# A Fourier mixing layer and a low-rank mixer in one kernel: batch 0's transposed operand by TensorE, batch 1's transform two slots on and interleaved, later steps moved

## The chip, the cores and the metric

The kernel runs on one core of one Trainium2 chip. The metric is the device time of one execution in microseconds (us), as the median of several runs. The core has five engines with a program each: TensorE (PE, with its weight loads as PEld), VectorE (DVE), ScalarE (ACT), GpSimd (POOL) and SyncE (SP), which issues most DMAs. They wait for each other by semaphores. An instruction that waits holds everything behind it on its engine.

## The reference

Batch 8, sequence 3136, width 256, all float32. `x` is Fourier-transformed along both axes and the real part kept; then a mixer follows that has a low-rank product along the sequence (rank 32) and two channel products (256 to 1024 to 256) with a relu between.

```python
X = np.fft.fft(x, axis=1)
X = np.fft.fft(X, axis=2)
x = X.real                                   # (8, 3136, 256)
xt = x.transpose(0, 2, 1)
h = xt @ U @ V                               # U: 3136 x 32, V: 32 x 3136
u = x + h.transpose(0, 2, 1)
ch = np.maximum(u @ w_ch1, 0.0) @ w_ch2
return u + ch
```

## The kernel before

**The transform of a batch.** The 3136 rows are folded on DVE with their mirror rows (`fold`: `alone`, `along_d`, `mirror`, `half`, `fourth`; tiles xf and xr hold the rows forward and reversed, eof, eor, eos, ge, gc and go the folded ones). The folded rows are multiplied on PE with tables of sines and cosines that the kernel makes itself. There are four such products per batch, each in two halves (`pn` 0 and 1): even cosine rows (`a` in `transform`), odd cosine rows (`c`), even sine rows (`s`) and odd sine rows (`d`). They collect in PSUM tiles `pt`; half 0 is copied out by ACT to a tile `ev`, and sums and differences of the two halves (`mirrored`, `apart`, `join`) go to the tiles A (cosine) and B (sine). From A and B, `chan(b, ch, h)` makes the transform along the width: a PSUM tile `pst`, copied to S (`h` 0) or T (`h` 1). Four pairs (`ch` 0 to 3) fill a batch's 1568 + 1 rows; the other half of the rows follows from them by symmetry.

**The low-rank part.** The products also yield the transform of U's columns, in the tile `tab`. `lowrank(b)` multiplies it with the width's table (`MDT`: MSN and MC) to `ptt`, 128 x 256. ACT copies that to TA (with two columns repaired) and a second time, as it is, to TX, and a transposing DMA on SP brings TX to TD. `hidden(b, hh)` multiplies TD with W1 to `pq`, copied to QF.

**The chunks.** The 8 x 1568 rows are worked in 25 chunks of 512. `front(c, hf)` makes a chunk's u for the rows (`hf` 0) and the mirrored rows (`hf` 1): two PSUM tiles `ph` from TA and V, added on DVE to S and T; a transposing DMA brings u to ut. `direct(c, q)` multiplies u with W1 into four PSUM tiles `p1`; ACT applies the relu (L722). `mirrors(c, q)` adds WD and DV products with QF to the same tiles for the mirrored rows, and ACT applies the relu again (L738). `second_product` multiplies with W2; DVE adds ut and writes `o` (L781, L782), POOL repairs two columns, and `store` sends it out. `odd_part` makes uo = S - T on DVE.

**PSUM.** Tag dft has two buffers, taken in turn by `pt` (of `even_rows` and `seq`), `ptt`, `pst`, `pq` and `ph`; p1 has four, p2 two.

**The order.** Up to `order.close()` the order is as written. After it, the order on PE and that of the folds on DVE is as written (`keep_in_program_order`), and a scheduler places the rest, ACT's and DVE's evictions, POOL's and SP's instructions, around them. Each chunk has six slots: `turn(c, 0)` to `turn(c, 5)`, so slot n is `turn(n // 6, n % 6)`. A table `due` says which steps of later batches' transforms stand in which slot. `transform(b)` gives a first slot and a list of steps per slot; the fold steps of batch b are spread over the slots from `last` on up to it; `chan` 2 and 3 stand in four slots from 6 * (b * 1568 // 512) on. The folds of batch b also issue the loads of batch b + 1 (`load_part`). `front(c + 1, 0)` stands between slots 4 and 5 of chunk c, `front(c, 1)` between slots 1 and 2; batch 1 is first needed by `front(3, 0)`, behind slot 16.

Every PE instruction of this part comes through the helper `mm` (L427), every fold through `fold_tt` (L422).

Of the kernel before, what the change touches and what calls it, by code (L numbers as in the profile page):

```python
# [11 lines left out]
FP32 = mybir.dt.float32  # L12
# [4 lines left out]
P = 128  # L17
# [9 lines left out]
QW = TE + NE  # L27
# [4 lines left out]
def kernel(  # L32
# [9 lines left out]
    nc = tc.nc  # L42
# [4 lines left out]
    HALF = S // 2  # L47
    CH = 512
# [4 lines left out]
    psum = ctx.enter_context(tc.tile_pool(name="psum", bufs=1, space=bass.MemoryType.PSUM))  # L53
# [58 lines left out]
    EB = 4  # L112
    BUFS = {"dft": 2, "p1": 4, "p2": 2}
# [5 lines left out]
    wp = ctx.enter_context(tc.tile_pool(name="wp", bufs=2))  # L119
# [74 lines left out]
    TD = [cpool.tile([P, 2, P], BF16, name=f"td{s}", tag=f"td{s}") for s in range(2)]  # L194
# [194 lines left out]
    def along_d(qs, src, dst, part):  # L389
        lo, hi = src[:, qs, :, 1:128], src[:, qs, :, 255:128:-1]  # L390
        if part == 0:
            fold_tt(dst[:, qs, :, 1:128], lo, hi, op=AL.subtract)
        else:
            fold_tt(dst[:, qs, :, 129:256], lo, hi, op=AL.add)

    def alone(qs, src, dst, eng=None):

        (eng or nc.gpsimd.tensor_copy)(dst[:, qs, :, 128:257:128], src[:, qs, :, 0:129:128])

    def mirror(nm, cols, op):  # L400
        if nm == 0:
            fold_tt(EOS[:, 0, :, :, cols], EOF_[:, 0:4:2, :, cols],
                                    EOR_[:, 3::-2, ::-1][:, :, :, cols], op=op)
        else:
            fold_tt(EOS[:, 1, :, :, cols], EOR_[:, 0:4:2, ::-1][:, :, :, cols],
                                    EOF_[:, 3::-2, :, cols], op=op)

    def half(b, par, cols):
        dst = GE if par == 0 else GO[b % 2]
        fold_tt(dst[:, :, :, cols], EOS[:, :, 0, :, cols], EOS[:, :, 1, :, cols],  # L410
                                op=AL.add if par == 0 else AL.subtract)

    def fourth(b, c, cols):
        fold_tt(GC[b % 2][c][:, :, cols], GE[:, 0, :, cols], GE[:, 1, :, cols],
                                op=AL.add if c == 0 else AL.subtract)
# [10 lines left out]
    def mm(*a, **k):  # L426
        ins = nc.tensor.matmul(*a, **k)  # L427
        if len(pinned) > 1:
            tc.keep_in_program_order(ins)
        if pinned:  # L430
            pinned.append(ins)
# [3 lines left out]
    def fold(b):  # L435

        for nm, (qf, qr) in enumerate(((EV, OD), (OD, EV))):
            yield lambda qf=qf: (alone(qf, xf, EOF_), along_d(qf, xf, EOF_, 0))
            yield lambda qf=qf: along_d(qf, xf, EOF_, 1)
            if b > 1:  # L440
                yield lambda qr=qr: (alone(qr, xr, EOR_), along_d(qr, xr, EOR_, 0))
                yield lambda qr=qr: along_d(qr, xr, EOR_, 1)
            if b + 1 < B:
                yield lambda qf=qf, qr=qr, nm=nm: load_part(b + 1, nm)
            yield lambda nm=nm: mirror(nm, slice(0, 128), AL.subtract)
            yield lambda nm=nm: mirror(nm, slice(128, 258), AL.add)
        yield lambda: half(b, 0, slice(0, 258))
        yield lambda: (fourth(b, 0, slice(0, 258)), fourth(b, 1, slice(0, 258)))
        yield lambda: half(b, 1, slice(0, 258))

    def load_part(b, nm):

        for q in (0, 2) if nm == 0 else (1, 3):
            load_f(x, xf, b, q, D)
        load_r(x, xr, b, 1 - nm, 2, D)
        if nm == 1:
            load_0(x, xf, xr, b, D)

    def state(b):

        if b not in ST:
            d = ST[b] = {}
            d["A"] = wp.tile([P, HALF + 1], BF16, tag="A", name="A", bufs=1)
            d["B"] = wp.tile([P, HALF + 1], BF16, tag="B", name="B", bufs=1)
            d["tab"] = wp.tile([P, 2, 2, P], BF16, tag="tab", name="tab", bufs=1)
            d["S"] = wp.tile([P, HALF + 1], BF16, tag="S", name="S", bufs=2)
            d["T"] = wp.tile([P, HALF + 1], BF16, tag="T", name="T", bufs=2)
        return ST[b]
# [79 lines left out]
    def even_rows(b, typ, pn, tag="dft"):  # L548

        d = state(b)  # L550
        ne = NE if b else 0
        if pn == 0:
            d["pt"] = psum.tile([P, QW], FP32, tag=tag, name="pt", bufs=BUFS[tag])
        pt = d["pt"]
        todo = products(b, 0, typ, P * typ, pn == 1, ne)
        if typ == 0:
            todo = todo + products(b, 0, 1, 256, pn == 0, ne)
        for n, (at, w, rhs) in enumerate(todo):
            mm(pt[:, at:at + rhs.shape[-1]], w, rhs, start=(pn == 0 and n == 0),
               stop=(n == len(todo) - 1), skip_group_check=True)  # L560
        if pn == 0:
            ev = d["ev"] = wp.tile([P, QW], FP32, tag="ev", name="ev", bufs=EB)
            nc.scalar.copy(ev[:, :TE + ne], pt[:, :TE + ne])
            return
        dst = d["A"] if typ == 1 else d["B"]
        nc.scalar.copy(strip(dst[:], 392, [[-2, NT + 1]]), pt[:, 0:NT + 1])
        nc.scalar.copy(strip(dst[:], 391, [[-2, NT]]), pt[:, NT + 1 + ne:TE + ne])
        if ne:
            nc.scalar.copy(d["tab"][:, typ, 0, :].rearrange("p (g r) -> p g r", r=R), four(pt, TE - NT))
# [7 lines left out]
    def mirrored(b, typ, kept):  # L577

        ne = NE if b else 0
        pt, ev = kept["pt"], kept["ev"]  # L580
        dst = ST[b]["A"] if typ == 1 else ST[b]["B"]
        nc.vector.scalar_tensor_tensor(strip(dst[:], 394, [[-1, 2], [2, NT]]),  # L582
                                       strip(ev[:], 1, [[NT + ne, 2], [1, NT]]), 2.0 if typ else -2.0,
                                       strip(pt[:], 1, [[NT + ne, 2], [1, NT]]),
                                       op0=AL.mult, op1=AL.subtract if typ else AL.add)
# [34 lines left out]
    def lowrank(b):  # L620
        d = ST[b]
        pt = psum.tile([P, 256], FP32, tag="dft", name="ptt", bufs=BUFS["dft"])
        parts = [(typ, par) for typ in range(2) for par in range(2 if b else 1)]
        for n, (typ, par) in enumerate(parts):
            mm(pt[:], d["tab"][:, typ, par, :], MDT[typ][:], start=(n == 0), stop=(n == len(parts) - 1))
        ta = TA[b % 2]
        nc.scalar.copy(ta[:], pt[:])
        nc.scalar.copy(ta[2 * R:, 0:P + 1:P], pt[2 * R:, P::-P])
        nc.scalar.copy(TX[:], pt[:])
        nc.sync.dma_start_transpose(out=TD[b % 2][:], in_=TX[:])  # L630

# [156 lines left out]
    def transform(b):  # L788

        def odd_rows(typ, pn):  # L790
            seq(b, 1, typ, pn)
            if pn:
                join(b, 1, typ)

        def even(typ, pn):
            even_rows(b, typ, pn)
            if pn:
                mirrored(b, typ, ST[b])

        a = [lambda pn=pn: even(1, pn) for pn in range(2)]  # L800
        s = [lambda pn=pn: even(0, pn) for pn in range(2)]
        c = [lambda pn=pn: odd_rows(1, pn) for pn in range(2)]
        d = [lambda pn=pn: odd_rows(0, pn) for pn in range(2)]
        rank = [lambda: lowrank(b)]
        ch = [lambda ch=ch, h=h: chan(b, ch, h) for ch in range(2) for h in range(2)]
        q = [lambda hh=hh: hidden(b, hh) for hh in range(2)]
        if b == 1:
            return 9, [a[:1], a[1:] + c[:1], c[1:], s, d, rank + ch[:1], ch[1:3], ch[3:] + q[:1], q[1:]]
        if b == 2:
            return 21, [[x] for x in a + c] + [d] + [[x] for x in s + rank + ch + q]  # L810
        return 6 * (b * HALF // CH) - 16, [[x] for x in a + c + s + d + rank + ch + q]

    CK = {}
    ST = {}
# [62 lines left out]
    pd = gen.tile([P, 2 * P], I32, name="pd", bufs=1)  # L877
# [11 lines left out]
    MDT = [MSN, MC]  # L889
# [85 lines left out]
    def spread_out(steps, lo, hi):  # L975
        for n, step in enumerate(steps):
            put(lo + (hi - lo) * n // len(steps), step)

    last = 5
    for b in range(1, B):  # L980
        e = 6 * (b * HALF // CH) - 2
        lo, (mid, steps) = last, transform(b)
        spread_out(list(fold(b)), lo, mid + (b == 1))
        for n, step in enumerate(steps):
            put(mid + n, *step)
        for n, (ch, h) in enumerate(((2, 0), (2, 1), (3, 0), (3, 1))):
            put(e + 2 + n, lambda b=b, ch=ch, h=h: chan(b, ch, h))
        last = mid + 1

    def turn(c, sl):  # L990
        for step in due.get(6 * c + sl, []):
# [84 lines left out]
```

## Time and profile before

| | |
|---|---|
| median of 3 runs | 477.37 us (476.77 to 477.91) |
| profiled execution, its own time | 478.38 us |
| its span, first to last instruction | 476.5 us |
| mean granted TensorE clock | 0.978 |
| PE busy | 439.5 us, 92% |
| DVE busy | 319.6 us, 67% |
| ACT busy | 297.0 us, 62% |
| chain that ended last: PE / DVE / ACT / DMA | 81% / 9% / 5% / 2% |

The page gives each engine's busy time, then the span in 40 equal slices of 11.9 us whose digits are tenths. A chain of what released what runs back from the last instruction. A wait is idle time of an engine right before an instruction, put down to what ended last. Matmuls are pipelined, so that PE's rows overlap, and the time from one start to the next is what a matmul takes of PE.

### The profile page before, as it was taken

What the parts mean: (1) busy time and instruction counts of PE and PEld (TensorE: products, weight loads), DVE (VectorE), ACT (ScalarE), POOL (GpSimd) and SP (SyncE); (2) the same over time, 40 slices, a digit from 0 to 9 for tenths busy, and PEclk for the clock granted to TensorE, in tenths of its full rate; (3) what the DMA queues carried; (4) which work ended last, traced back from release to release, by engine and by line L of the source; (5) the groups of instructions that cost most, each with busy time, mean ns of one, the idle gap of its engine ahead of it and who ended that gap; (6) DMA issues with size and microseconds to landing.
All of it is one profiled execution on the core that took longest, in us unless ns stands there. A gap on an engine that the chain in (4) does not pass through costs nothing.

```text
span 476.5 us, 8933 instructions
## 1 busy us (share of the span) xinstructions
PE 439.5 (92%) x3263; PEld 286.6 (60%) x3310; DVE 319.6 (67%) x649; ACT 297.0 (62%) x635; POOL 123.9 (26%) x340
## 2 busy tenths in 40 slices
PE   4795977999999999999999999999999999999995
PEld 1572344665666666666666756666665666666674
DVE  8974697886975776766776697586777544434542
ACT  6944553486467765767657755776576756666551
POOL 8550162243314421322132321231122100110111
PEclk9969898999999999999999999999999999999999
DMA  5899286975738648493958564695234343335353
GB/s 162 217 232 168 33 255 144 191 168 150 207 102 178 186 99 178 108 236 104 218 77 238 109 195 109 74 236 142 80 80 103 89 112 74 110 89 146 104 128 114
DMA packets 91519, 68.39 MB, mean 144 GB/s; under 512 B 57758, under 2 KB 84786, under 8 KB 91474
## 3 DMA queue, kind: packets, MB, share of 16 engines
q1 hardware_dynamic: 86002, 53.45, 47.7%
q0 software_dynamic: 5472, 14.36, 12.5%
q8 instruction: 26, 0.43, 0.5%
q14 instruction: 19, 0.16, 0.1%
HBM read 28.86 MB, written 25.69 MB: 114 GB/s over the span
## 4 chain that ended last, share of the span: by engine, by line
PE 81%; DVE 9%; ACT 5%; DMA 2%; issue 1%; POOL 0%; DVEq 0%; POOLq 0%
PE p L427 60%; PE pt L427 10%; PE pst L427 4%; PE ph L427 2%; DVE u L679 2%; DMA td<-tx 2%; DVE eof L422 2%; PE pq L427 2%; PE pu L295 1%; ACT S L618 1%; PE ptt L427 1%; PE fill L871 1%; DVE B L582 1%; DVE pho L205 1%; DVE ge L422 1%
## 5 line engine op out<-in xcount | busy, mean ns | idle before, releaser
L427 PE MATMUL p<-w,h 128*128 128x256 bf16 x1576 | 189.7, 274 | 0.5 <-DVE o L782 0.5
L427 PEld LDWEIGHTS <-h 128*128 128x128 bf16 x1576 | 150.4, 98 | 42.3 <-issue 18.1
L738 ACT ACTIVATE h<-p 128x512 bf16<-128x512 f32 (+1 forms) x200 | 101.5, 595 | 44.4 <-PE p L427 42.2
L722 ACT ACTIVATE h<-p 128x512 bf16<-128x512 f32 (+1 forms) x200 | 101.7, 598 | 21.2 <-PE p L427 21.1
L781 DVE TENSOR_TENSOR o<-p,ut 128x256 f32<-128x256 f32 x99 | 41.6, 420 | 91.7 <-PE p L427 72.3
L427 PE MATMUL p<-u,w 128*128 128x512 bf16 (+1 forms) x355 | 91.1, 374 | 4.2 <-DVE u L679 1.3
L786 POOL TENSOR_TENSOR o<-o,fx 128x2 f32<-128x2 f32 (+1 forms) x99 | 44.9, 454 | 159.0 <-issue 81.2
L427 PEld LDWEIGHTS <-w 128*128 128x128 bf16 x400 | 38.9, 97 | 41.7 <-issue 4.1
L427 PE MATMUL p<-uo,wd 128*128 128x512 bf16 (+1 forms) x199 | 51.5, 379 | 0.5
L57 POOL DMA_INDIRECT xf<-in_x_dram,xidx x32 | 35.4, 1105 | 21.8 <-DVE eof L422 8.3
L782 DVE TENSOR_TENSOR o<-p,ut 128x256 f32<-128x256 f32 x99 | 40.9, 413 | 0.0
L679 DVE TENSOR_TENSOR u<-ph,T 128x512 bf16<-128x512 f32 (+8 forms) x64 | 35.0, 558 | 4.9 <-PE ph L427 3.6
L422 DVE TENSOR_TENSOR eof<-xf 99x1016 bf16<-99x1016 f32 x32 | 38.2, 1206 | 0.0
L422 DVE TENSOR_TENSOR eor<-xr 99x1016 bf16<-99x1016 f32 x32 | 37.9, 1207 | 0.0
L679 DVE TENSOR_TENSOR u<-ph,S 128x512 bf16<-128x512 f32 (+8 forms) x64 | 35.0, 557 | 1.7 <-PE ph L427 1.3
L695 POOL TENSOR_TENSOR fx<-ut 128x4 f32<-128x4 bf16 x50 | 13.4, 269 | 85.3 <-DMA ut<-u 85.3
L427 PE MATMUL pt<-te,gc 98*128 98x229 bf16 (+1 forms) x192 | 25.3, 268 | 5.4 <-DVE gc L422 4.4
L427 PEld LDWEIGHTS <-wd 128*128 128x128 bf16 x200 | 19.7, 98 | 17.1 <-issue 1.7
L618 ACT CAST S<-pst 128x392 bf16<-128x392 f32 (+1 forms) x31 | 19.0, 613 | 15.3 <-PE pst L427 15.2
L427 PEld LDWEIGHTS <-go 98*128 98x128 bf16 x216 | 20.3, 101 | 13.3 <-issue 6.6
L427 PEld LDWEIGHTS <-gc 98*128 98x128 bf16 x216 | 19.8, 100 | 11.1 <-DVE gc L422 5.3
L427 PE MATMUL pt<-to,go 98*128 98x424 bf16 (+1 forms) x96 | 21.0, 357 | 3.7 <-DVE u L679 3.7
(151 smaller groups left out, 442.7 us busy)
## 6 DMA issues: line engine op xcount, KB each, us to landing
out_dram<-o SPq DMA_DIRECT2D x33, 512.0 KB
xr<-in_x_dram SPq DMA_DIRECT2D x14, 784.0 KB
out_dram<-o SPq DMA_DIRECT2D x8, 384.0 KB
out_dram<-o SPq DMA_DIRECT2D x9, 256.0 KB
xr<-in_x_dram SPq DMA_DIRECT2D x1, 1568.0 KB
out_dram<-o SPq DMA_DIRECT2D x8, 128.0 KB
ut<-u SPq DMA_TRANSPOSE x50
vv<-vv SPq DMA_DIRECT2D x3, 196.0 KB
```

Of the source, the lines that this page charges most:

```text
L57: nc.gpsimd.indirect_dma_start(out_, None, bass.AP(t.tensor, t.offset, [[w, rows], [1, w]]), bass.IndirectOffsetOnAxis(idx, 0), element_of ...
L205: nc.vector.tensor_single_scalar(y, y, 2 ** bits - 1, op=AL.bitwise_and)
L422: ins = nc.vector.tensor_tensor(*a, **k)
L427: ins = nc.tensor.matmul(*a, **k)
L618: nc.scalar.copy(to, pt[:, :n])
L679: nc.vector.tensor_tensor(u[:, s, at:at + hi - lo], phs[s][:, at:at + hi - lo], src, op=AL.add)
L695: nc.gpsimd.tensor_tensor(fx[:, :, 1], ut[:, 0:n, 0] if hf else ut[:, n:2 * n, 0], ut[:, n + 1:2 * n + 1, 0], op=AL.subtract)
L722: nc.scalar.activation(k["h", 0][q][:, j - 4 * q, :w], p1[:, :w], AF.Relu)
L738: nc.scalar.activation(k["h", 1][q][:, g, :w], k["p1"][g][:, :w][:, ::-1], AF.Relu)
L781: nc.vector.tensor_tensor(o[:, ts, 0:P], p2[:, :w, 0:P], ut[:rows, ts, 0:P], op=AL.add)
L782: nc.vector.tensor_tensor(o[:, ts, P:D], p2[:, :w, P:D], strip(ut[:rows], (CH // P + t0 + 1) * P, [[P, w], [-1, P]]), op=AL.add)
L786: nc.gpsimd.tensor_tensor(o[:, ts, cols], o[:, ts, cols], fx[:rows, ts, 1 - hf:], op=AL.add)
```

## The change

It has four parts.

- `lowrank(0)` no longer copies ptt to TX and sends it through the transposing DMA. Four matmuls with the width's table as the stationary operand and `tab` as the moving one make the transposed product in a PSUM tile `ptd` (tag p2), and ACT copies that to TD. Batches 1 to 7 keep the DMA.
- Batch 1's transform begins in slot 11 instead of 9 and takes seven slots instead of nine: even and odd sine rows share two slots (s0 with d0, s1 with d1), and the low-rank step stands with all four first `chan` in slot 16, both `hidden` in slot 17. Its folds keep slots 5 to 10. `even_rows` and `mirrored` get keys of their own, `pe` and `ve`, so that an even product may be half done while an odd one is made.
- Batch 2's transform begins in slot 23 instead of 21 and ends in slot 35 instead of 34, with some steps sharing a slot; its folds are spread over slots 16 to 22 instead of 10 to 20.
- Batches 3 to 7 begin one slot later, and the first half of the odd sine rows comes before the even ones (d0, s0, s1, d1). Their folds move by one slot or two.

```diff
@@ even_rows, mirrored
-            d["pt"] = psum.tile([P, QW], FP32, tag=tag, name="pt", bufs=BUFS[tag])
-        pt = d["pt"]
+            d["pe"] = psum.tile([P, QW], FP32, tag=tag, name="pt", bufs=BUFS[tag])
+        pt = d["pe"]
...
-            ev = d["ev"] = wp.tile([P, QW], FP32, tag="ev", name="ev", bufs=EB)
+            ev = d["ve"] = wp.tile([P, QW], FP32, tag="ev", name="ev", bufs=EB)
...
-        pt, ev = kept["pt"], kept["ev"]
+        pt, ev = kept["pe"], kept["ve"]
@@ lowrank
         nc.scalar.copy(ta[2 * R:, 0:P + 1:P], pt[2 * R:, P::-P])
+        if b == 0:
+            pd = psum.tile([P, 2, P], FP32, tag="p2", name="ptd", bufs=BUFS["p2"])
+            for s in range(2):
+                for typ in range(2):
+                    mm(pd[:, s, :], MDT[typ][:, s * P:(s + 1) * P], d["tab"][:, typ, 0, :], start=(typ == 0),
+                       stop=(typ == 1))
+            nc.scalar.copy(TD[0][:], pd[:])
+            return
         nc.scalar.copy(TX[:], pt[:])
         nc.sync.dma_start_transpose(out=TD[b % 2][:], in_=TX[:])
@@ transform
         if b == 1:
-            return 9, [a[:1], a[1:] + c[:1], c[1:], s, d, rank + ch[:1], ch[1:3], ch[3:] + q[:1], q[1:]]
+            return 11, [a[:1], a[1:] + c[:1], c[1:], [s[0], d[0]], [s[1], d[1]], rank + ch, q]
         if b == 2:
-            return 21, [[x] for x in a + c] + [d] + [[x] for x in s + rank + ch + q]
-        return 6 * (b * HALF // CH) - 16, [[x] for x in a + c + s + d + rank + ch + q]
+            return 23, [a[:1], a[1:] + c[:1], c[1:], s[:1], s[1:] + d[:1], d[1:], rank, ch[:1], ch[1:2],
+                        ch[2:3], ch[3:], q[:1], q[1:]]
+        return 6 * (b * HALF // CH) - 15, [[x] for x in a + c + d[:1] + s + d[1:] + rank + ch + q]
@@ the table of slots
         lo, (mid, steps) = last, transform(b)
-        spread_out(list(fold(b)), lo, mid + (b == 1))
+        spread_out(list(fold(b)), lo, mid - (b == 1))
...
-        last = mid + 1
+        last = max(16, mid + 1)
```

## The prediction

> **What bounds the kernel now.** I read the page's busy times and its slices first, then the waits, the chain in order of time, the timelines of TensorE (PE) and VectorE (DVE), and windows of 1 and 2 us where PE stands idle.
>
> ```profile
> PE 439.5 (92%) x3263; PEld 286.6 (60%) x3310; DVE 319.6 (67%) x649; ACT 297.0 (62%) x635; POOL 123.9 (26%) x340
> ...
> PE   4795977999999999999999999999999999999995
> ...
> PEclk9969898999999999999999999999999999999999
> ```
>
> PE is the bound, and from slice 8 on (after 95 us) it is full. What can be won lies mostly before 95 us, where PE's digits and its clock dip together. The waits (total, times, longest) say why:
>
> ```profile
> DVE S L616 <- PE pst L427: 6.7, 1, 6.7
> ...
> PE pq L427 <- DMA td<-tx: 4.8, 1, 4.8
> ...
> PE pt L427 <- DVE gc L422: 4.4, 1, 4.4
> ```
>
> The chain puts them in order of time (start, length):
>
> ```profile
> 36.87 10.72 DMA td<-tx
> 47.63 1.89 PE pq L427 x4
> ...
> 69.86 1.22 DVE eos L422 x2
> 71.11 1.24 DVE ge L422
> ```
>
> Batch 0's transposing DMA takes from 36.87 to 47.6; `hidden` stands in PE's order and holds everything behind it, `chan(0, 3, ..)` too, whose copies DVE needs before it can begin batch 1's folds (51.53). DVE then works almost without a gap to 74.84, and batch 1's first transform matmul at slot 9 waits for it until 73.15. After both waits the granted clock is at half (PEclk, the third figure from the end of each line):
>
> ```profile
> 45.00:46.00 1.00, 0.00 (x0) 0.00 (x0) 0.00 (x0) 0.00 (x0) 0.00 (x0) 0.75 0.96 116
> ...
> 48.00:49.00 1.00, 1.00 (x4) 0.42 (x3) 0.00 (x0) 0.30 (x1) 0.00 (x0) 0.50 0.74 49
> ...
> 53.00:54.00 1.00, 0.54 (x4) 0.29 (x3) 0.84 (x4) 1.00 (x3) 0.00 (x0) 1.00 0.00 0
> ```
>
> In the steady part little is left, per batch of 51.8 us (PE's waits, 172 to 224 us):
>
> ```profile
> PE pt L427 <- DVE u L679: 0.6, 1, 0.6
> PE pst L427 <- DVE u L679: 0.3, 1, 0.3
> ```
>
> A third, of 0.43, hides in a merged row: two `ph` matmuls take 0.81 us (232.78) where they otherwise take 0.38.
>
> **The change, part by part.** I take the new order of each engine, which the built program shows, and follow it with durations from the rows at full clock: a second product's 16 matmuls 1.75 us, `direct` 1.73, WD 0.96, DV 0.23, `chan` 0.33, `even` of two halves 0.79, a fold of xf or xr 1.13, a pair of o 0.7, a pair of u 1.3.
>
> *Transposed operand.* One DMA goes; four matmuls with 128 columns come. None is in the trace: the nearest row, `ptt` with 256 columns, starts 0.11 apart, `fill` with 392 columns 0.165, the 32-column `ptu` below 0.05. So 0.2 to 0.66; I take 0.4, near `ptt`. They stand before `fill` and delay all `chan` by that. ACT's copy to td replaces the copy to tx, same shape, 0.37: nothing. `hidden` now waits for ACT's copy of `chan(0, 2, 0)`, which ended at 43.51, so 43.9, instead of 47.63: 3.7 won. From there to `front(0, 1)` PE took 5.12 at half clock; at full it is 0.87 + 0.66 + 0.96 + 0.23, and 0.5 waiting for ACT's copies: 3.2, so 1.9 more. The relus behind it begin at 47.1 instead of 52.94, and DVE's last copy ends at 46.8 instead of 51.64. ACT and PE take turns from there, so all runs **5.85** earlier. The transposes of ut lose a DMA ahead of them in SP's queue (1.31 to issue); they were no bound, since DVE first reads ut at 64.3, and it landed by 50.1.
>
> *Batch 1 two slots on.* DVE's folds keep their slots 5 to 10 and end at 74.84 - 5.85 = 69.0. PE does a second product, WD and DV, `front(2, 0)` and one more second product instead of waiting, and is at slot 11 at 67.9 (68.79 - 5.85 = 62.9, then 1.75 + 0.96 + 0.23 + 0.32 + 1.75). The wait is not gone: both PSUM buffers of tag dft now hold `front(2, 0)`'s ph, and its evictions stand on DVE behind go (69.0) and a pair of o (69.7); the first ends at 70.3. New stall 2.4 where 4.36 was. With the half clock from 72.8 to 77 also gone (a0 0.97 instead of 0.40, the second product 2.77 instead of 1.75): 4.36 + 1.6 - 2.4 = **3.6 won**. The waits at 82.62 (1.48) and 86.63 (0.60) go too, as no fold of batch 2 stands between batch 1's joins any more, against 0.2 before `direct`: **1.9 won**.
>
> *Even and odd interleaved, low rank and four `chan` in slot 16.* s0, d0, s1, d1 cost PE the same (the keys `pe` and `ve` only keep two half-done results apart). In slot 16 five PSUM results pass through two buffers. The second `chan` needs ptt's, which ACT has read three times (ta, the two-column fix, tx), with an S copy in between: 1.15 of waiting, and 0.35 at the fourth: **1.5 lost**. Both `hidden` of batch 1 come one second product and a `front` later (93.45); their DMA is issued behind the store of chunk 1's second half on SP, at about 88.9. In the trace one issued at 97.16 was there by 100.21, so 92.0 without the store; its 512 KB at the 290 GB/s of 64 to 72 us are 1.8 more: 0 to 0.6, I take **0.3 lost**. Behind it on PE wait `direct(3, 0)` and everything else.
>
> *Batch 2's folds in slots 16 to 23 instead of 10 to 21.* Some 16 us of DVE in 20 us that also hold about 7 of u, o and uo. Following the order, PE begins `direct(3, 0)` at 94.35 (104.34 in the trace) and comes to slot 23 at 109.6. DVE has no gap from 99 on: two folds 2.3, u 1.5, o 0.7, a fold 1.15, eos 1.4, ge 1.15, o 0.75, gc 1.2, go 1.15, and the first u of `front(4, 0)` 0.65, at 111.0. So a0 waits 1.4 for that buffer, with 0.4 in small waits before it. The loads of batch 3 that go with these folds (gathers on POOL, xr on SP) move from slots 12 and 17 to 17 and 20; they are first read in slot 24, over 11 us later, where a gather lands in 6.7 (the page's DMA issues): nothing. The waits at 112.39 (0.47) and 121.80 (0.60) go: **0.7 lost**.
>
> *Batch 2's transform.* c1's joins stand on DVE behind two folds of xf (2.3) and a pair of o, and `front(4, 1)` needs the buffer that they free: WD and DV end at 117.9. On ACT the copies of a1 come behind four relus and end at 115.05; on DVE follow A's mirrored half (to 115.65), eh 0.55, the folds 2.3, o 0.7 and the joins 1.2: 120.4. **2.5 lost**, less 0.3 that the trace has at that `front` (129.80): 2.2.
>
> *Later batches.* One slot on, odd sine before even. a1 is followed by `front` after only 1.2 us of mirrors, and that needs a1's buffer: 0.35 to 0.6; the same behind d1: 0.1 to 0.4; the evictions before c0, s0 and rank come within 0.2 of their readers. I get 0.65 to 1.3 per batch against 1.3 (1.8 where batch 6 and 7 are folded): between 0 and 0.9 won, in four batches with folds. I take **1.5 won**; bounds -2.5 and +4.
>
> Sum: 5.85 + 3.6 + 1.9 - 1.5 - 0.3 - 0.7 - 2.2 + 1.5 = 8.2 (8.15). The profiled execution took 478.38 us, a span of 476.5 and 1.9 around it; it becomes 470.2. The median of the runs is 1.0 below it, 477.37, so I forecast **469.2**.
>
> *A rule to weigh.* PE's waits of 4.75 and 4.36 us halved the clock, the one of 1.48 (81.1 to 82.6) did not; this change makes two of 2.4, between those rows. I take the clock as kept, since it fell some 2.8 us after PE stopped at 42.7 and 4 us after it stopped at 68.8. The Trainium skill, "TensorE: Matmul & The Clock Gate", section "Part 1: The HAM clock gate", says that the clock drops after an idle window of about 3.4 us that runs free of the program; by that rule 2.4 us keep it and the sum stays. The trace agrees at 4.4 and at 1.5 us; no run here shows 2.4.
>
> **The rivals.** 0.2%, about 0.95 us, is what a measurement of this kernel can tell from no change.
>
> *The new stalls halve the clock.* Each is followed by some 4 us at half (72.8 to 77), so 2 lost twice: 473.2. For it: half of such a stall falls into whatever the clock watches. Against: the row of 1.48.
>
> *Batch 1's rows aren't there yet.* DVE now wants xr at 46.8; its landing isn't shown. The td DMA, issued behind it on the same queue, landed at 47.6, which speaks for at most 0.8. The w2 load took 18.7 us and landed near 49.7, and DMA still moved 176 GB/s at 47 us. If xr came with it, DVE's chain would be 2.3 later, the stall at slot 11 4.7, and the clock lost again (1.6): 3.9 back, 473.1.
>
> *DVE becomes the bound: slower.* What batch 2 pays at its `front` (2.4, joins behind folds on DVE) recurs once in each of the four later batches whose transform stands among folds (3 to 6): 4 x 2.4 = 9.6 lost, and the 1.5 of the steady part not won, so 9.6 - 6.65 = 3.0 slower, 480.3. It decides from 1.7 us a batch on, where 4 x 1.7 takes the 6.65 won elsewhere. For it: DVE is 37.5 of 52 us busy there, and the interleaved order has less between a `front` and the result whose buffer it needs. Against: in the order of batch 3 on a single fold stands before those joins, not two.
>
> *The steady part gives all its waits back.* The upper bound of that term, 2.5 more: 466.7.
>
> **The numbers.** Forecast, 467 to 471.5: 0.58. Clock 0.10, late rows 0.12, steady gain 0.09, DVE-bound 0.09, gains and losses that cancel within 0.2%: 0.02. Faster is the sum of the first four, 0.89; same 0.02; slower 0.09. The range leaves out the slower case and the cancelling one, and takes in the steady term's bounds (2.5 below, 4.0 above the forecast) and 1.7 for the sizes of the other terms: 465 to 475.
>
> **What would show it.** Right: no wait for td at `pq` near 43 us; PEclk 1.0 from 45 to 80; DVE's first fold of xr near 47; go ending near 69; stalls at PE pt behind u of about 2.4 (slot 11), 1.4 (slot 23) and at a ph of 2.5 (batch 2); three ACT copies before the second pst of slot 16. Wrong: a wait DVE eor <- DMA xr, PEclk at 0.5 after 67 us, or waits of PE on DVE in the steady windows over 1.5 us a batch.

## The result, and the profile after

The changed kernel takes **470.55 us** (468.14 to 472.09), the kernel before, run on the same chip, 477.64 (476.77 to 478.32). The ratio is 0.9852, interval 0.9817 to 0.9888: 7.1 us less where 8.2 were forecast. The forecast of 469.2 and its range held, but in part by luck: the start won less than forecast and the later batches three times as much, and the two errors nearly cancelled. Ratios and their intervals, here and below, leave out executions that took over 1.5% more than the fastest of their kernel; only e10 and e11 have such. The profiled execution took 472.09 us, span 470.3, granted clock 0.975.

The page's busy times, slices and clock:

```profile
PE 442.2 (94%) x3267; PEld 290.2 (62%) x3314; DVE 319.6 (68%) x649; ACT 297.1 (63%) x635; POOL 129.9 (28%) x340
...
PE   4897897998899999999999999999999999999995
...
PEclk9858998999899999999999999999999999999999
```

PE's digits are fuller before slice 8, and the two long dips are gone. The clock still dips, in three places after the setup, one of them new (slice 10, counted from 0, about 125 us). PE's waits in the whole span (total, times, longest):

```profile
PE pt L427 <- DVE u L687: 3.4, 2, 2.4
PE ph L427 <- DVE tab L545: 2.1, 1, 2.1
...
PE fill L880 <- ACT td L635: 1.1, 1, 1.1
PE pst L427 <- ACT S L618: 1.1, 2, 0.7
```

The waits for td by DMA (4.8) and gc (4.4) are replaced by one of 2.4 and one of 2.1, both forecast, and by one of 1.1 that was not. From 172 us on PE waits for nothing. PE's timeline (start, length, what, and in brackets the idle time before it) at the places that the change touches:

```profile
36.98 0.22 PE L427 MATMUL ptd<-tab,msn 128*128 128x128 bf16 x1
...
38.46 1.16 PE L880 MATMUL fill<-to 98*128 98x392 bf16 x6 [1.09 <-ACT td L635]
...
47.91 1.02 PE L427 MATMUL pq<-w,td 128*128 128x512 bf16 x4 [0.35 <-ACT S L618]
...
74.59 0.93 PE L427 MATMUL pt<-te,gc 98*128 98x229 bf16 x4 [2.37 <-DVE u L687]
...
93.95 0.33 PE L427 MATMUL pst<-A,mc 128*128 128x393 bf16 x1 [0.70 <-ACT S L618]
...
116.01 0.56 PE L427 MATMUL pt<-te,gc 98*128 98x229 bf16 x4 [1.04 <-DVE u L687]
...
125.06 0.39 PE L427 MATMUL ph<-vv,ta 32*128 32x512 bf16 x1 [2.10 <-DVE tab L545]
```

The first two lines show what was missed: the four `ptd` matmuls start 0.055 us apart, 0.22 in all, but `fill` behind them waits 1.09 until ACT has copied ptd. Both take buffers of tag p2, and of its two the other is held. After the two long stalls (2.37 and 2.10) PE goes on at half clock: the four matmuls at 74.59 take 0.93, where the same four at 116.01, behind a stall of 1.04, take 0.56.

**Where the time went.** The two profiled executions can't be laid over each other from their starts: in the setup, which the change does not touch, the first `ptt` matmul comes at 35.21 before and at 36.77 after, since half clock lasted 10.2 us there in the one and 13.7 in the other. Counted from that matmul, the relus of equal rank (the first of before with the first of after, and so on) tell what each stretch won. The last column is experiment e4 below, the changed kernel without the wait of `fill`.

| stretch, up to the | forecast | after | e4 |
|---|---|---|---|
| first relu of chunk 0's mirrored rows | 5.85 | 3.1 | 5.5 |
| first relu of chunk 3 (slots 11 to 17) | 3.6 + 1.9 - 1.5 - 0.3 = 3.7 | 3.1 | 4.6 |
| last relus of chunk 6 (batch 2) | -0.7 - 2.2 = -2.9 | -3.05 | -3.0 |
| last relu | 1.5 | 4.5 | 4.5 |
| sum | 8.15 | 7.7 | 11.6 |

The 7.7, less 1.56 for the setup, are the 6.2 by which the spans differ (476.5 and 470.3). Two cautions go with the table. Its border after chunk 6 cuts the two kernels differently: the first half of batch 3's odd cosine rows (0.39 of PE) stands ahead of it in before and behind it in after, so that batch 2 lost 0.4 more, and the later batches won 0.4 more, than the rows say. And the first row hangs on one execution of before. From the first `ptt` matmul to that relu its profile has 17.7 us, with a wait of 4.8 for td; the profiles of e2, e3, e3s, e3o, e8 and e9, which have the same start, have 14.0 to 16.7, with waits of 1.9 to 4.0. Against a usual execution the start wins less than the table shows.

### The profile page after: what moved, and what is told of

It is laid out like the page before. It is cut to its first block, busy times and chain, and to the rows that moved or that the text cites. A ratio compares the mean times of both kernels' runs of the same rounds, so it can differ in the third digit from the quotient of the medians.

```text
span 470.3 us, 8944 instructions
## 1 busy us (share of the span) xinstructions
PE 442.2 (94%) x3267; PEld 290.2 (62%) x3314; DVE 319.6 (68%) x649; ACT 297.1 (63%) x635; POOL 129.9 (28%) x340
## 4 chain that ended last, share of the span: by engine, by line
PE 84%; DVE 7%; ACT 6%; issue 2%; POOL 0%; DVEq 0%; POOLq 0%
PE p L427 63%; PE pt L427 10%; PE pst L427 4%; PE ph L427 3%; DVE eof L422 1%; PE pu L295 1%; PE pq L427 1%; DVE u L687 1%; ACT h L730 1%; PE fill L880 1%; DVE A L582 1%; PE ptt L427 1%; DVE pho L205 1%; ACT A L566 1%; ACT S L618 0%
## 5 line engine op out<-in xcount | busy, mean ns | idle before, releaser
L427 PE MATMUL p<-u,w 128*128 128x512 bf16 (+1 forms) x361 | 93.4, 381 | 3.8 <-DVE u L687 0.7
L427 PE MATMUL p<-uo,wd 128*128 128x512 bf16 (+1 forms) x198 | 50.5, 374 | 0.4
L703 POOL TENSOR_TENSOR fx<-ut 128x4 f32<-128x4 bf16 x50 | 16.4, 327 | 65.8 <-DMA ut<-u 65.7
L427 PE MATMUL ph<-vv,ta 32*128 32x512 bf16 (+15 forms) x128 | 23.5, 325 | 2.8 <-DVE tab L545 2.1
L702 POOL TENSOR_TENSOR fx<-ut 128x4 f32<-128x4 bf16 x25 | 6.0, 240 | 70.3 <-DMA ut<-u 70.3
```

The costliest lines, as they stand in the source:

```text
L702: nc.gpsimd.tensor_tensor(fx[:, :, 0], ut[:, n:2 * n, 0], ut[:, 0:n, 0], op=AL.subtract)
L703: nc.gpsimd.tensor_tensor(fx[:, :, 1], ut[:, 0:n, 0] if hf else ut[:, n:2 * n, 0], ut[:, n + 1:2 * n + 1, 0], op=AL.subtract)
```

## The experiments

Ratios are to the kernel before on the same chip, with its interval.

**e1: the operand alone.** The kernel before with only the new branch of `lowrank`.

```diff
+        if b == 0:
+            pd = psum.tile([P, 2, P], FP32, tag="p2", name="ptd", ...)
...
+            nc.scalar.copy(TD[0][:], pd[:])
+            return
```

> Only batch 0's operand by TensorE; every slot as before. Theory (the wait for td was on the path, and DVE's folds follow it): PE waits no more for td, DVE's go of batch 1 ends about 3 us earlier than 74.8 (after a start that is equally long), the wait of 4.4 for gc at slot 9 stays, and nothing changes after 95 us: 3 faster, 474 to 475. Rival (the folds of batch 1 are bound by their loads, so the wait only moves to slot 9): the wait for gc grows to 7 or more, 477 to 478.

Measured 474.27 (473.79 to 475.21), ratio 0.9924 (0.9906 to 0.9943), 3.4 less than the 477.66 of the kernel before, run beside it. PE's waits:

```profile
PE pt L427 <- DVE gc L422: 4.4, 1, 4.4
...
PE fill L879 <- ACT td L635: 1.1, 1, 1.1
```

The wait for gc is as long as ever: what the start wins alone does not shorten it, since DVE's folds and PE move together. The wait of `fill` belongs to this part of the change.

**e2: the moves alone.** The changed kernel with batch 0's operand by the DMA again.

```diff
-        if b == 0:
-            pd = psum.tile([P, 2, P], FP32, tag="p2", name="ptd", ...)
...
-            return
```

> The change without its first part: batch 0's operand still by the transposing DMA, all moves of batches 1 to 7 made. Theory (late part independent of the start): the wait for td of 4.8 is back, the stall at slot 11 is 2.4 behind u, at batch 2's front 2.1, and from 160 us on PE has no waits on DVE, worth some 5 us: 472 to 474. Rival (the late gain needs the earlier start): the late waits are back, 476 to 478.

Measured 472.92 (471.35 to 475.18), ratio 0.9899 (0.9871 to 0.9927). `pq` waits 2.0 for td again, not the 4.8 expected from the profile of before; the stalls of 2.4, 1.0 and 2.1 are there, those of the steady part are not. Operand and moves win 3.4 and 4.7 alone, 8.1 in sum, and 7.1 together; with executions of these kernels up to 4 us apart, that difference shows no interaction.

**e3: the late batches alone.** The kernel before with the later slot and the new order of batches 3 to 7. In this run and in e3s, e3o, e8 and e9 the keys `pe` and `ve` come with it; the diffs leave that out.

```diff
-        return 6 * (b * HALF // CH) - 16, [[x] for x in a + c + s + d + rank + ch + q]
+        return 6 * (b * HALF // CH) - 15, [[x] for x in a + c + d[:1] + s + d[1:] + rank + ch + q]
```

> Only batches 3 to 7: one slot later and d0 before s; batches 0 to 2 as before. Theory (these batches lose about 1 us each to second-hand waits of PE on DVE's u, and the new order takes them away by itself): same until 170 us, then no waits of PE on DVE, 4.5 to 5 faster, about 473. Rival (what batches 1 and 2 do sets the phase of the later ones): the waits of 0.6 and 0.3 per batch stay, within 1 us of 477.6.

Measured 472.87 (471.37 to 473.57), ratio 0.9896 (0.9876 to 0.9915): 4.8 less, three times the 1.5 that was forecast for it. A batch takes 50.85 us instead of 51.81, and PE waits for nothing from 172 us on.

**e3s and e3o: slot and order, each alone.**

```diff
 e3s: return 6 * (b * HALF // CH) - 15, [[x] for x in a + c + s + d + rank + ch + q]
 e3o: return 6 * (b * HALF // CH) - 16, [[x] for x in a + c + d[:1] + s + d[1:] + rank + ch + q]
```

> Batches 3 to 7 one slot later, in the old order of steps (s0, s1, d0, d1); batches 0 to 2 as before. Theory A (the waits went since another step now stands behind each front: c0, s0 and rank instead of c1, d0 and the first chan; the slot alone does that at two of three places): most of the 4.6 of the run with both, 473 to 474.5, with waits of PE on DVE's u of at most 0.3 a batch. Theory B (it is the order of d0 before s that counts): the waits of 0.9 a batch stay, 477.

> Batches 3 to 7 with d0 before s, at their old slots; batches 0 to 2 as before. Theory A (the slot counts): the wait of 0.6 behind a front for c1 stays, and so does 0.3 for the first chan: 476.5 to 477.5. Theory B (the order counts): 473 to 474.

Measured 478.71 (477.53 to 480.25), ratio 1.0023 (1.0004 to 1.0041), and 481.8 (481.64 to 482.23), ratio 1.0078 (1.0065 to 1.0091). Neither part alone is a gain, so neither of the two expectations held. PE's waits from 172 to 460 us say why. Before:

```profile
PE pt L427 <- DVE u L679: 2.5, 5, 0.6
PE pst L427 <- DVE u L679: 1.2, 4, 0.3
PE p L427 <- DVE u L679: 0.8, 2, 0.5
```

With the slot alone:

```profile
PE ph L427 <- DVE u L679: 4.7, 5, 1.2
```

With the order alone:

```profile
PE ph L427 <- DVE u L679: 4.2, 5, 0.8
PE pt L427 <- DVE u L679: 2.5, 5, 0.6
PE pst L427 <- DVE u L679: 1.0, 3, 0.3
PE p L427 <- DVE u L679: 0.8, 2, 0.5
```

The later slot takes all 4.5 of the waits of before away, and each part alone brings a new one, at the second of two `ph`, five times. PE's timeline of e3s shows what surrounds it:

```profile
175.84 0.96 PE L427 MATMUL pt<-te,gc 98*128 98x229 bf16 x8
...
177.84 0.38 PE L427 MATMUL ph<-vv,ta 32*128 32x512 bf16 x1
179.10 0.37 PE L427 MATMUL ph<-vv,ta 32*128 32x512 bf16 x1 [0.89 <-DVE u L679]
...
181.16 0.96 PE L427 MATMUL pt<-te,gc 98*128 98x229 bf16 x8
```

The two halves of the even sine rows (`te,gc` at 175.84 and 181.16) stand around the `front`. They add to one `pt`, which keeps one of the two dft buffers from the first to past the second; the two `ph` in between must share the other, and the second waits for DVE's u of the first. In the order a, c, s, d one slot later, and in the order a, c, d, s, s, d at the old slot, the sine halves fall on both sides of `front(c, 1)`. With both parts together, as with neither, they fall on one side.

**e8 and e9: is it the held buffer?** e3s and e3o with both even sine halves in one slot behind the `front`.

```diff
 e8 (from e3s): ... - 15, [[x] for x in a + c] + [[], s] + [[x] for x in d + rank + ch + q]
 e9 (from e3o): ... - 16, [[x] for x in a + c + d[:1]] + [[], s] + [[x] for x in d[1:] + rank + ch + q]
```

> Kernel before with batches 3 to 7 one slot later in the old order (as e3s, which took 478.71), but both halves of the even sine rows in one slot, behind front(c, 1) instead of around it. Theory H (the held buffer): an even product keeps one of the two dft buffers from its first half to its mirrored copy; where a front stands between the halves, its two ph must share the other one, and the second waits about 1 us for DVE's u of the first. Then e8 has no wait of 1 us at a ph from 170 us on, a period of 50.8 to 51.2 us a batch, and 473 (472 to 475). Theory O (the order of odd and even sines itself matters, by what DVE has queued): the odd sine rows still come last, the wait stays, 478 to 479.

> Kernel before with the odd sine rows' first half ahead of the even ones at the old slot (as e3o, which took 481.8), but both halves of the even sine rows in one slot behind front(c, 1). Theory H (the held buffer): the wait of 1.0 us at the second ph goes, those of 0.7 at c1 and 0.5 at the first chan stay, as in the kernel before: 477 to 478.5. Theory O: 481 to 482.

Measured e8 475.55 (473.84 to 476.89), ratio 0.9932 (0.9909 to 0.9955); e9 479.53 (477.28 to 481.08), ratio 1.0028 (1.0008 to 1.0048). Both lie between the two theories' numbers, e8 0.5 and e9 1.0 above the range that the held buffer gives. The waits tell them apart all the same. Those at `ph` are gone in both, as the held buffer says and the other theory does not; in e8 this is all that is left from 172 to 460 us, and e9 has the same line beside the waits of the kernel before:

```profile
PE pt L427 <- ACT ev L563: 3.0, 5, 0.6
```

The second half, now right behind the first, writes to the tile that ACT is still copying out, 0.6 each time. This price was left out of the expectation; it is more than the miss in either.

**e4: the filler first.** The changed kernel with the six filler matmuls ahead of `ptd` instead of behind it.

```diff
         if b == 0:
+            filler("p2")(6)
             pd = psum.tile([P, 2, P], FP32, tag="p2", name="ptd", bufs=BUFS["p2"])
...
-    filler("p2")(6)
```

> The changed kernel with the six filler matmuls ahead of the four new ones instead of behind them, so that the filler needn't wait for ACT's copy out of the buffer that both share. Theory (that wait of 1.1 and the small gaps after it cost a window at half clock near 44 us): the wait goes, PEclk stays 1.0 from 34 to 72 us, 2.5 faster than the changed kernel, about 468. Rival (the half clock comes from later small gaps): only the wait goes, about 469.5, with 0.5 in PEclk near 44 us as before.

Measured 468.65 (468.06 to 470.01), ratio 0.9811 (0.9789 to 0.9833), 1.9 less than the changed kernel, against the same kernel before. PE's timeline:

```profile
37.00 1.16 PE L881 MATMUL fill<-to 98*128 98x392 bf16 x6
...
45.56 1.02 PE L427 MATMUL pq<-w,td 128*128 128x512 bf16 x4 [0.68 <-ACT S L618]
```

`fill` waits no more, and `pq` begins 8.78 after the first `ptt` (36.78) instead of 11.14 (36.77 to 47.91). Of those 2.4, some 1.0 are the wait (e1, which has the wait and kept the clock, is 1.04 behind e4 at the first relu of the mirrored rows) and the rest the half clock that after has there and this execution has not. The start now wins 5.5 in the table, where 5.85 were forecast. That the wait brought the half clock about, as the theory says, is not shown: 468.65 lies between the two numbers expected, e1 has the wait and no half clock, and e5 below, with the filler first, has half clock in the start without the wait:

```profile
39.14:42.55 3.41, 3.25 (x8) 1.12 (x8) 2.45 (x6) 1.53 (x3) 0.00 (x0) 0.50 1.20 204
```

(PE's busy time comes first behind the length of the window; the granted clock is the third figure from the end.)

**e5: batch 3's folds two slots later.** e4, with batch 2's joins no longer behind two folds on DVE.

```diff
-        last = max(16, mid + 1)
+        last = max(16, mid + 1) + 2 * (b == 2)
```

> The changed kernel with the filler first, and batch 3's folds from slot 26 on instead of 24, so that no fold stands on DVE ahead of batch 2's c1 joins. Theory (the wait of 2.1 at front(4, 1) is those two folds and what stands with them): it falls to 0.3 or less, and the window at half clock behind it goes too: 2 to 3.5 faster than the filler-first run (468.65), 465.2 to 466.7. Rival (later folds collide with batch 3's transform, which needs them by slot 39): the wait comes back as a wait for gc or u near 160 to 170 us, 468 to 469.

Measured 464.9 (463.01 to 466.92), ratio 0.9737 (0.9718 to 0.9756). That is 3.75 less than e4, a little more than expected. The wait of 2.1 is gone, and so is the half clock behind it. Counted as in the table, the stretch of batch 2 goes from 3.0 lost to 1.0 won.

**e7: batch 1's last fold later too.** e5, with the fold go of batch 1 in slot 11.

```diff
-        spread_out(list(fold(b)), lo, mid - (b == 1))
+        folds = list(fold(b))
+        spread_out(folds[:-1] if b == 1 else folds, lo, mid - (b == 1))
+        if b == 1:
+            put(mid, folds[-1])
```

> As the run with later folds, and batch 1's last fold (go) put into slot 11, behind front(2, 0), so that the evictions of its ph don't stand behind go on DVE. Theory (the stall of 2.4 at slot 11 is DVE's queue: go 1.15 and a pair of o): go leaves it, uo (0.34) comes into it, so the stall falls to about 1.6; 0.8 faster than the run with later folds alone, and 1.7 more in the executions whose clock falls there. Rival (a0 waits for gc, not for the buffer): the stall stays at 2.4, no difference.

Measured **464.56** (462.73 to 465.43), ratio 0.9717 (0.9698 to 0.9735). It is the lowest median of all, 6 us below the changed kernel, but only 0.3 below e5's, with overlapping intervals: the 0.8 expected is not shown in the times. It is in PE's wait at slot 11, which falls from 2.4 to 1.6, as the theory of DVE's queue says and the rival does not:

```profile
PE pt L427 <- DVE u L688: 2.6, 2, 1.6
```

**e10 and e11: matmuls in the stall.** e5 and e7 with six matmuls of 392 columns, whose product nobody reads, ahead of batch 1's first transform matmul.

```diff
+    def busy():
+        pt = psum.tile([P, 2 * NT], FP32, tag="p1", name="busy", bufs=BUFS["p1"])
+        for _ in range(6):
+            mm(pt[:], TABO[0][:PQ, 0, 1, 0:P], TABO[0][:PQ, 0, 0, 0:2 * NT], start=True, stop=True)
...
-            return 11, [a[:1], a[1:] + c[:1], c[1:], [s[0], d[0]], [s[1], d[1]], rank + ch, q]
+            return 11, [[busy] + a[:1], a[1:] + c[:1], c[1:], [s[0], d[0]], [s[1], d[1]], rank + ch, q]
```

> Kernel e5 (which took 464.9, 463.01 to 466.92, granted clock .982 to .987 over its runs) with six matmuls of 392 columns, 1.0 us, into a p1 buffer ahead of batch 1's first transform matmul, where PE waits 2.4 us for DVE; their product is not used. Theory W (the clock goes by the share of a window of 3.41 us, on a grid fixed for each execution, in which PE streams: in the traces so far every window under 0.37 was followed by half clock, none over 0.46): the wait falls to 1.4, the window's share stays over 0.46 wherever the grid falls, no half clock at slot 11 in the profile, and 463.5 to 464.9 with a clock that is not lower than e5's. Rival F (the matmuls cost their own time, because p1 is not free there or its rotation delays direct(2, 0)): 465.5 to 466.

> Kernel e7 (464.56, 462.73 to 465.43, clock .983 to .989; wait at slot 11 of 1.6) with the same six matmuls of 392 columns ahead of batch 1's first transform matmul. Theory W: the wait falls to 0.6, no half clock at slot 11, 463 to 464.6; what spread is left comes from the setup and the stretch before 45 us, which the matmuls do not touch. Rival F: 465 to 465.6.

Measured 465.99 (462.11 to 470.78), ratio 0.9725 (0.9694 to 0.9756), and 467.26 (462.58 to 472.62), ratio 0.976 (0.9714 to 0.9807): no gain shown. Five of the twelve executions took over 469 us; the medians of the others are 465.05 and 464.19, as in e5 and e7. The profile of e10 is one of those; that of e11 (462.58) is not, and its relus, counted from the first `ptt`, lie within 0.04 us of e7's from the first to the last, so there the matmuls cost nothing, against the rival, and bring nothing, since e7's profile had no half clock at slot 11 either. In e10:

```profile
PE pq L427 <- DMA td<-tx: 4.1, 1, 4.1
PE pt L427 <- DVE u L688: 2.4, 2, 1.4
```

The stall is 1.4 and the clock stays full at slot 11, both as expected, but `hidden` of batch 1 waits 4.1 for its transposing DMA, and half clock follows at 99.3. There POOL issued a gather 0.3 us before that DMA (93.45 and 93.75); in e7's profile it came 0.9 behind it (88.89 and 89.76). Whether the matmuls bring this about, and whether the other four executions have the same wait, stays open.

## Why the prediction was right, and where it was not

**The mechanism of the start was right, one cost beside it was missed.** The step "So 0.2 to 0.66; I take 0.4" priced the four matmuls, which took 0.22, but not the buffer that they hold: `fill` comes next in the same tag and waits 1.09 for ACT's copy. With that wait gone (e4), 5.5 of 5.85 are there. The half clock that after has from 43.53 on cost 1.3 more (e1, with the same wait at full clock, is that much ahead of it at the first relu of the mirrored rows); it does not hang on the wait alone, as e1 and e5 show. And "5.85" itself is more than its parts (3.7 and 1.9 are 5.6), and it was read from an execution with an unusually long start (17.7 us where the six others have 14.0 to 16.7); by the medians of e1 the operand wins 3.4, the wait of `fill` included.

**"I take the clock as kept" was wrong in the profiled execution, at both stalls.** "PEclk at 0.5 after 67 us", which the forecast named as a sign of being wrong, came. These windows of after are cut where its clock changed:

```profile
40.11:43.53 3.42, 2.09 (x9) 0.66 (x7) 2.50 (x5) 1.07 (x2) 0.00 (x0) 1.00 0.96 196
43.53:46.94 3.41, 3.15 (x8) 1.24 (x9) 1.74 (x4) 1.99 (x4) 0.00 (x0) 0.50 1.63 156
70.83:74.25 3.42, 1.39 (x13) 1.09 (x12) 3.42 (x6) 1.48 (x4) 0.41 (x3) 1.00 1.22 201
74.25:77.66 3.41, 2.85 (x9) 1.47 (x10) 1.88 (x5) 1.52 (x3) 0.39 (x2) 0.50 1.31 82
122.03:125.45 3.42, 1.32 (x9) 0.28 (x8) 3.42 (x8) 2.06 (x4) 2.60 (x4) 1.00 1.68 187
125.45:128.86 3.41, 3.41 (x17) 2.45 (x18) 1.88 (x3) 0.00 (x0) 2.33 (x6) 0.50 0.71 241
```

The first window of each pair, in which PE has little to do, is followed by one at half clock: behind stalls of 2.37 and 2.10, and behind a window in which no gap was over 0.44. The price at slot 11 is 1.5: e4, whose clock held there, wins 4.6 in that stretch and after 3.1. The rival with 473.2 thus happened in its mechanism, at some 1.5 each instead of 2; the steady part paid for it. The Trainium skill, "TensorE: Matmul & The Clock Gate", section "Part 1: The HAM clock gate", puts the drop after an idle window of about 3.4 us that runs free of the program. The length and the free running agree with the trace; that the window is idle does not, as the first window of each pair shows PE at work for 1.3 to 2.1 us of 3.4. The forecast said that the trace of before agreed at 4.4 us, where the window was empty. At its other long wait, of 4.75, the same trace spoke against the rule: PE had worked for 0.80 us of the window, and half clock followed at 45.49:

```profile
42.08:45.49 3.41, 0.80 (x5) 0.27 (x3) 0.77 (x2) 1.43 (x3) 0.00 (x0) 1.00 1.54 98
```

**"New stall 2.4 where 4.36 was" was right:** 2.37. The waits behind it went as forecast. "1.5 lost" in slot 16 was near: the view of waits has one there, 0.70 for the S copy at 93.95, but by the starts of the matmuls the three gaps between the four `chan` (92.92 to 93.95, 94.12 to 94.52, 94.69 to 95.14, where 0.165 is usual) add up to 1.4. The 0.3 at batch 1's `hidden` did not come: in after `pq` begins at 98.73 without a wait. In e10's profile, though, it was 4.1.

**Batch 2 was right in kind, and in size by luck.** a0 waited 1.04 (1.4 forecast) and the `front` 2.10 (2.5). Half clock behind the `front`, put at nothing, made up for it: the 16 matmuls of a second product took 3.35, from 125.38 to 128.73, where 1.75 is usual. So 3.05 were lost where 2.9 were written. e5 shows that the cause named for the `front`, joins behind two folds on DVE, is the cause.

**"I take 1.5 won" for the later batches was the term most mis-sized:** 4.5, above its bound of 4. The step that failed is "I get 0.65 to 1.3 per batch" of new waits. By the starts of the matmuls there were none over 0.25 (172 to 460 us): all 4.5 of the old waits went and nothing of that size came in their place. The forecast also did not see why slot and order belong together (e3s, e3o). It looked at each wait by itself, and by that either might have been moved without the other, which loses 1 and 4 us. The rival that the steady part gives all its waits back, put at 466.7, is what happened there.

**The remaining rivals.** DVE did not become the bound: PE has no wait from 172 us on. Batch 1's rows were not late: all 32 eor folds together idle 0.2 for xr in the page of after.

## What to carry to other kernels

Where a buffer is held across other work that uses the same tag, the slots in which it is taken and given back must stand on the same side of that work; a move by one slot, or a change of order, can be a loss alone and a gain together. When a new result borrows a buffer, look at who takes the next one of that tag, not only at what the new instructions cost. Price a short stall of TensorE with the clock it may lose in a sparse window, not only with its own length. A gain that is read from a wait in one profile is as uncertain as that wait: here the wait for td was 1.9 to 4.8 in seven profiles of the same start.

## What the hardware showed that was not expected

All changes of the granted clock in these traces lie on a grid of 3.413 us whose start differs from one execution to the next. For the 14 profiled executions I added up, per window of that grid, the time in which PE streams columns (0.215 us per 512 columns, from the starts of matmuls, without the tails that the busy time contains). Of some 1780 windows at full clock, 29 had PE streaming for less than 0.375 of the window, and 28 of these were followed by half clock (the other begins at 7 us, where PE had hardly begun); about 15 lay between 0.375 and 0.47, and 9 of them were; above that none was. The two bounds were drawn after the event, and a matmul whose record is missing from a trace takes 0.06 off a share. By this, a stall of 2.4 us loses the clock or not by where the grid cuts it. In e5 the same stall of 2.37 (68.35 to 70.72) falls on a boundary at 69.81, and the shares are 0.49 and more:

```profile
66.40:69.81 3.41, 1.95 (x18) 1.58 (x17) 3.38 (x6) 2.04 (x4) 0.74 (x2) 1.00 1.11 264
69.81:73.22 3.41, 2.50 (x16) 1.54 (x16) 2.54 (x6) 1.91 (x5) 0.61 (x4) 1.00 1.28 133
```

Nearly all of this is read from the traces after the event. In one place a run set the share on purpose: in e10 the stall at slot 11 and the six added matmuls fall into the window from 68.58 to 71.99. PE streams for 0.60 of it, and without the six it would be 0.31; the clock stayed full.

```profile
68.58:71.99 3.41, 2.25 (x18) 1.55 (x16) 3.41 (x6) 1.34 (x3) 0.27 (x3) 1.00 1.26 205
```

That is one execution; in e11 the share would have been 0.56 without them, so it shows nothing here. The reading goes with the spread of the runs: the four of the changed kernel have mean clocks of 0.975, 0.975, 0.982 and 0.985 and take 472.09, 471.61, 469.48 and 468.14 us.
